# Attention scores computed one head at a time on 64-row, 32-column parts of the TensorE array

## The chip, the core and the metric

The kernel runs on one core of one Trainium2 chip. The metric is device time in microseconds (us) of one execution; lower is better. The engines named below are PE (TensorE, the matrix engine; its weight loads are the separate track PEld), DVE (VectorE), ACT (ScalarE), POOL (GpSimd) and SP (SyncE, which here only issues transfers).

## What is computed

A chunked attention is followed by a gated feed-forward layer. The attention has 4 batches, 8 heads, 768 positions and a head size of 64. Every chunk of 32 queries sees 8 memory keys, 16 keys to the left of the chunk, its own 32 and 8 to the right, 64 keys in all. Everything is float32.

```python
scores = scale * np.matmul(q_c, k_full.transpose(0, 1, 3, 2))   # per chunk: 32 queries x 64 keys
scores = scores - np.max(scores, axis=-1, keepdims=True)
a = np.exp(scores)
a = a / (np.sum(a, axis=-1, keepdims=True) + 1e-09)
out[:, :, c_start:c_end] = np.matmul(a, v_full)
...
xn = x / rms * rms_g                     # x: 3072 tokens x 512
g = xn @ w_gate                          # 512 x 1536
silu = g * (1.0 / (1.0 + np.exp(-g)))
val = xn @ w_val
return (silu * val @ w_out)              # 1536 x 512
```

## The kernel before

Tokens are worked in 8 blocks of 384 (`HT`). The attention of a block is 4 units (`units`, 32 in all); a unit is one batch, one half of the sequence and one pair of heads, so 12 chunks (`NC`) of 32 queries for two heads.

One unit goes through these stages. `stage_ta` and `stage_tb` (L287, L292) transpose queries and keys with DVE into `qb` and `kw` (in the later blocks these are parts of the tiles `qp` and `kv`). `stage_tc` (L300, L301) copies neighbouring keys with ACT. `stage_s` (L309) multiplies queries by keys into the PSUM tile `s`. `stage_ma` and `stage_mb` take the maximum `mx` (L330) and subtract it into `pe` (L336) on DVE, `stage_e` (L341) takes the exponential on ACT, `stage_p` (L348) transposes the result on PE into `pT`, `stage_c` copies that into `pt` (also part of `qp`), and `stage_o` (L368) multiplies by the values into `o`. The two heads of a pair lie on top of each other: head 0 on partitions 0 to 63, head 1 on 64 to 127.

In `qb` the queries of a chunk are 128 partitions by 64 columns: columns 0 to 31 are head 0 and hold numbers on partitions 0 to 63 only, columns 32 to 63 are head 1 and hold numbers on partitions 64 to 127 only. The rest is zero, set once at the start. So one multiplication over 128 partitions gives both heads' scores. `s` has four quarters of 32 partitions: chunks whose `par` is 0 write partitions 0 to 63, those whose `par` is 1 write 64 to 127; `par` changes after every two chunks.

The operands are plain float32, and every multiplication of `stage_s` shows in the trace as two weight loads (LDWEIGHTS) and two MATMULs: 12 chunks give 24 of each for a unit.

The feed-forward part takes its weights and activations as pairs of rounded halves (`xh`, `xl`, `wh_*`, `wl_*`): `moe_in` (L561) makes `pg` and `pv` with 12 MATMULs each, `moe_out` (L599) adds 9 MATMULs into `po` for the step before, and `moe_h` makes `t`, `hh` and `hl` (L568, L572, L575, L584, and the copy in L227) on ACT and DVE.

The first two blocks' attention (8 units) runs in an order that is written out token by token (`ORDER`); its PE also runs multiplications of zeros (`warm`, L307) between the stages. From then on a scheduler orders the work: attention of the next block is put into the feed-forward of the current one in visits (`attn_visits`), and the instructions of PE keep their program order (`on_pe`). A visit runs, on PE, `stage_p` of the unit before, `stage_s` of this unit and `stage_o` of the unit two before, as far as there is one. So of the 4 score stages of a later block two are followed at once by `stage_o`. The scheduler orders DVE and ACT by the dependences that it sees between tiles.

Of the kernel before, what the change touches and what calls it, by code (L numbers as in the profile page):

```python
# [19 lines left out]
CH = 32  # L20
LC, RC = 16, 8
KC = NM + LC + CH + RC
# [45 lines left out]
def tile_kernel(ctx: ExitStack, tc: tile.TileContext, q, k, v, mem_k, mem_v,  # L68
                w_gate, w_val, w_out, rms_g, out):
    nc = tc.nc  # L70
# [35 lines left out]
    def on_pe(ins):  # L106
        if pinned:
            tc.keep_in_program_order(ins)

    def psum_a(name):  # L110
        return psa.tile([P, 512], F32, name=name, tag="at")
# [22 lines left out]
    def which(u):  # L134

        return 1 + u % 2 if u < NE else 0
# [172 lines left out]
    def stage_s(u):  # L309
        d = st[u]  # L310
        qb = qbs[which(u)]
        s = psum_a(f"s{u}")
        hf = units[u][1]
        kw = d["kw"][:, hf:hf + NC]
        for c in range(NC):
            i, par, cp = c // 4, (c // 2) % 2, c % 2
            o = (2 * i + cp) * KC
            on_pe(nc.tensor.matmul(s[64 * par:64 * par + 64, o:o + KC],  # L318
                             lhsT=qb[:, c].rearrange("p s q -> p (s q)"), rhs=kw[:, c], start=True, stop=True))
        d["s"] = s  # L320

    def stage_m(u):
# [357 lines left out]
    for e in range(2):  # L680
        r = slice(64 * e, 64 * e + 64)
# [6 lines left out]
    def attn_visits(blk, x):  # L688


        us = list(range(blk * NG, (blk + 1) * NG))
        for n in range(NG + 2):
            with tc.high_priority():
                if 1 <= n <= NG:
                    stage_p(us[n - 1])
                if n < NG:
                    u = us[n]
                    stage_s(u)
                if n >= 2:
                    stage_o(us[n - 2])  # L700
                    stage_r(us[n - 2], x)
                if n < NG:
                    stage_m(u)
                    stage_e(u)
                if 1 <= n <= NG:
                    stage_c(us[n - 1])
                if n < NG and u + 1 < len(units):
                    stage_t(u + 1)
            if n >= 2 and us[n - 2] + 1 < len(units):
                load_v(us[n - 2] + 1)  # L710
            if n < NG and u + 2 < len(units):
                load_qk(u + 2)
            yield
        with tc.high_priority():
            stage_n(x)
        yield
# [75 lines left out]
    def tok_o(n):  # L792
# [10 lines left out]
        V=lambda n, e=None: stage_v(n, e or ("d" if n < NG else "a")),  # L803

        S=stage_s, M=stage_ma, a=stage_mb, E=stage_e, P=stage_p,
        C=lambda n, e="a": stage_ch(n, 0, e), m=lambda n, e="a": stage_ch(n, 1, e),
        O=stage_o, X=stage_ra, x=stage_rb, u=tok_u,
# [121 lines left out]
```

## Time and profile before

| | us |
|---|---|
| median of 3 runs (732.32 to 733.74) | 733.04 |
| the profiled execution | 731.54 |
| its span, first to last instruction | 729.8 |
| PE busy in the span | 715.1 (98%) |
| DVE busy | 380.0 (52%) |
| ACT busy | 287.8 (39%) |
| POOL busy | 36.4 (5%) |

PE is busy in nearly the whole span, but MATMULs overlap in the records: a record is longer than the distance to the next one's start. What a stage costs is read from where the next stage starts, not from the sum of its records. The 32 score stages have 768 MATMULs, of which the 24 later units have 576.

### The profile page before, as it was taken

What the parts mean: (1) busy time and instruction counts of PE and PEld (TensorE: products, weight loads), DVE (VectorE), ACT (ScalarE), POOL (GpSimd) and SP (SyncE); (2) the same over time, 40 slices, a digit from 0 to 9 for tenths busy, and PEclk for the clock granted to TensorE, in tenths of its full rate; (3) what the DMA queues carried; (4) which work ended last, traced back from release to release, by engine and by line L of the source; (5) the groups of instructions that cost most, each with busy time, mean ns of one, the idle gap of its engine ahead of it and who ended that gap; (6) DMA issues with size and microseconds to landing.
All of it is one profiled execution on the core that took longest, in us unless ns stands there. A gap on an engine that the chain in (4) does not pass through costs nothing.

```text
span 729.8 us, 13052 instructions
## 1 busy us (share of the span) xinstructions
PE 715.1 (98%) x5136; PEld 656.6 (90%) x5136; DVE 380.0 (52%) x725; ACT 287.8 (39%) x600; POOL 36.4 (5%) x143
## 2 busy tenths in 40 slices
PE   8889999999999999999999999999999999999997
PEld 7778999999989999899999999989998999999996
DVE  4888999865645443444535353445434543332222
ACT  4899676643452323422333232432234222341112
POOL 3300000001000000000000000000000000000000
PEclk8999999999999999999999999999999999999999
DMA  8994563414412320122212123021311210010001
GB/s 173 203 259 141 173 202 116 132 37 102 85 37 68 55 50 22 62 46 42 43 38 66 23 45 61 20 66 31 66 29 34 64 32 20 20 44 0 1 1 43
DMA packets 143173, 50.20 MB, mean 69 GB/s; under 512 B 126984, under 2 KB 134536, under 8 KB 143112
## 3 DMA queue, kind: packets, MB, share of 16 engines
q1 hardware_dynamic: 139832, 44.49, 26.6%
q10 hardware_dynamic: 3280, 4.88, 1.8%
q8 instruction: 40, 0.66, 0.4%
q14 instruction: 21, 0.17, 0.1%
HBM read 43.06 MB, written 6.29 MB: 68 GB/s over the span
## 4 chain that ended last, share of the span: by engine, by line
PE 92%; ACT 3%; DMA 3%; DVE 1%; issue 0%; POOL 0%; ACTq 0%; SPq 0%; POOLq 0%
PE pv L561 28%; PE po L599 28%; PE pg L561 27%; PE s L318 3%; PE o L368 3%; PE xT L440 1%; PE pT L348 1%; DMA ws<-in_moe_w_val_dram 1%; DMA memV<-in_mem_v_dram 1%; DMA vw<-in_v_dram 1%; ACT junk L398 0%; ACT ws L508 0%; ACT pt L227 0%; DMA kv<-in_v_dram 0%; ACT qb L227 0%
## 5 line engine op out<-in xcount | busy, mean ns | idle before, releaser
L561 PE MATMUL pv<-xh,wh_v 128*128 128x384 f32 x384 | 132.8, 346 | 0.0
L561 PE MATMUL pg<-xh,wh_g 128*128 128x384 f32 x384 | 129.7, 338 | 0.7 <-DVE t L572 0.7
L561 PE MATMUL pv<-xh,wl_v 128*128 128x384 f32 x384 | 129.5, 337 | 0.6 <-DVE wl_v L532 0.6
L561 PE MATMUL pg<-xh,wl_g 128*128 128x384 f32 x384 | 129.5, 337 | 0.0
L561 PE MATMUL pg<-xl,wh_g 128*128 128x384 f32 x384 | 129.3, 337 | 0.0
L561 PE MATMUL pv<-xl,wh_v 128*128 128x384 f32 x384 | 129.3, 337 | 0.0
L572 DVE SCALAR_TENSOR_TENSOR t<-t,pg 128x384 f32<-128x384 f32 x96 | 53.1, 553 | 138.6 <-ACT t L568 138.5
L227 ACT CAST hh<-t 128x384 fp32r<-128x384 f32 x95 | 48.7, 512 | 174.9 <-PE po L599 165.3
L599 PE MATMUL po<-wh_o,hh 128*128 128x512 f32 x285 | 113.8, 399 | 0.3
L599 PE MATMUL po<-wh_o,hl 128*128 128x512 f32 x285 | 113.1, 397 | 0.0
L599 PE MATMUL po<-wl_o,hh 128*128 128x512 f32 x285 | 112.1, 393 | 0.0
L584 DVE TENSOR_TENSOR hl<-t,hh 128x384 fp32r<-128x384 f32 x95 | 52.9, 557 | 100.7 <-ACT hh L227 95.7
L568 ACT ACTIVATE t<-pg 128x384 f32<-128x384 f32 x96 | 47.2, 492 | 135.9 <-PE pg L561 130.8
L575 DVE TENSOR_TENSOR t<-t,pv 128x384 f32<-128x384 f32 x95 | 52.5, 552 | 64.9 <-PE pv L561 64.4
L561 PEld LDWEIGHTS pg<-xh,wh_g 128*128 128x128 f32 x384 | 72.1, 188 | 4.4 <-DVE t L572 0.9
L561 PEld LDWEIGHTS pg<-xl,wh_g 128*128 128x128 f32 x384 | 72.1, 188 | 3.6
L561 PEld LDWEIGHTS pv<-xh,wh_v 128*128 128x128 f32 x384 | 72.1, 188 | 2.4
L561 PEld LDWEIGHTS pv<-xh,wl_v 128*128 128x128 f32 x384 | 72.2, 188 | 0.9 <-DVE wl_v L532 0.9
L561 PEld LDWEIGHTS pv<-xl,wh_v 128*128 128x128 f32 x384 | 72.2, 188 | 0.3
L561 PEld LDWEIGHTS pg<-xh,wl_g 128*128 128x128 f32 x384 | 72.1, 188 | 0.0
L599 PEld LDWEIGHTS po<-wh_o,hl 128*128 128x128 f32 x285 | 53.5, 188 | 14.1 <-DVE hl L584 1.8
L599 PEld LDWEIGHTS po<-wh_o,hh 128*128 128x128 f32 x285 | 53.5, 188 | 10.0 <-ACT hh L227 1.7
(112 smaller groups left out, 772.9 us busy)
## 6 DMA issues: line engine op xcount, KB each, us to landing
kn<-in_k_dram SPq DMA_DIRECT2D x96, 52.0 KB
qn<-in_q_dram SPq DMA_DIRECT2D x96, 48.0 KB
out_dram<-ob ACTq DMA_DIRECT2D x18, 256.0 KB
ws<-in_moe_w_gate_dram SPq DMA_DIRECT2D x4, 1024.0 KB
ws<-in_moe_w_val_dram SPq DMA_DIRECT2D x4, 1024.0 KB
ws<-in_moe_w_out_dram SPq DMA_DIRECT2D x4, 1024.0 KB
kv<-in_v_dram SPq DMA_DIRECT2D x48, 84.0 KB
kv<-in_v_dram SPq DMA_DIRECT2D x48, 70.0 KB
```

The source lines that it names most:

```text
L227: return nc.scalar.copy(out, in_)
L318: on_pe(nc.tensor.matmul(s[64 * par:64 * par + 64, o:o + KC], lhsT=qb[:, c].rearrange("p s q -> p (s q)"), rhs=kw[:, c], start=True, stop= ...
L348: on_pe(nc.tensor.transpose(out=t[:, i * P:(i + 1) * P], in_=pe[:, i * P:(i + 1) * P], identity=ident))
L368: on_pe(nc.tensor.matmul(o[64 * par:64 * par + 64, c0:c0 + D + 1], lhsT=pt[:, i, 2 * par + hh].rearrange("p c q -> p (c q)"), rhs=d["v"][: ...
L440: on_pe(nc.tensor.transpose(out=t[:, i * P:(i + 1) * P], in_=tiles[i][:, kt * P:(kt + 1) * P], identity=ident))
L561: on_pe(nc.tensor.matmul(ps[:, 0:HT], lhsT=weight(a, n, f, kt), rhs=xs[c][:, kt], start=cnt == 0, stop=cnt == 3 * NKT - 1))
L568: nc.scalar.activation(t, g, AF.Tanh, scale=0.5)
L572: nc.vector.scalar_tensor_tensor(out=t, in0=t, scalar=1.0, in1=g, op0=ALU.add, op1=ALU.mult)
L575: nc.vector.tensor_tensor(out=t, in0=t, in1=vv, op=ALU.mult)
L584: nc.vector.tensor_tensor(out=hl, in0=t, in1=hh.bitcast(F32), op=ALU.subtract)
L599: on_pe(nc.tensor.matmul(po[i], lhsT=h[a][:, i * P:(i + 1) * P], rhs=weight(c, "o", f), start=f == 0 and n == 0, stop=f == NF - 1 and n == 2))
```

## The change

`stage_s` no longer multiplies both heads at once. For each chunk it issues two multiplications, one for each head. Head `hh` reads partitions 64·`hh` to 64·`hh`+63 of keys and of its own 32 query columns, and writes 32 partitions of `s`, the same ones as before. The numbers in `s` are those of before; the zeros in `qb` are no longer read.

```diff
         for c in range(NC):
             i, par, cp = c // 4, (c // 2) % 2, c % 2
             o = (2 * i + cp) * KC
-            on_pe(nc.tensor.matmul(s[64 * par:64 * par + 64, o:o + KC],
-                             lhsT=qb[:, c].rearrange("p s q -> p (s q)"), rhs=kw[:, c], start=True, stop=True))
+            for hh in range(2):
+
+                r, w = slice(64 * hh, 64 * hh + 64), 64 * par + 32 * hh
+                on_pe(nc.tensor.matmul(s[w:w + CH, o:o + KC], lhsT=qb[r, c, hh], rhs=kw[r, c], start=True, stop=True))
         d["s"] = s
```

So the four quarters of `s` now belong to four parts of the array: rows 0 to 63 with columns 0 to 31 (head 0, `par` 0), rows 64 to 127 with columns 32 to 63 (head 1, `par` 0), rows 0 to 63 with columns 64 to 95 (head 0, `par` 1) and rows 64 to 127 with columns 96 to 127 (head 1, `par` 1). Before there were two parts: all rows with columns 0 to 63 and all rows with columns 64 to 127. Lines after L318 move down by two or three.

On PE the stages keep their places. The third visit of the first scheduled block shows it; `pT` is `stage_p`, `s` is `stage_s`, `o` is `stage_o`, and `po` is the feed-forward's output. Before:

```order
L348 MATMUL pT_2178<-ident,pe_2112 128x128 x3
L318 MATMUL s_2182<-kv,qp 64x64 x12
L368 MATMUL o_2195<-kv,qp 64x65 x12
L599 MATMUL po_1031<-wh_o_1310,hh 128x512
L599 MATMUL po_1031<-wl_o_1311,hh 128x512
```

The changed kernel at the same place:

```order
L350 MATMUL pT_2298<-ident,pe_2232 128x128 x3
L321 MATMUL s_2302<-kv,qp 32x64 x24
L370 MATMUL o_2327<-kv,qp 64x65 x12
L601 MATMUL po_1127<-wh_o_1406,hh 128x512
L601 MATMUL po_1127<-wl_o_1407,hh 128x512
```

The row of `s` has 24 multiplications with 32 output partitions instead of 12 with 64; nothing stands in another place.

On DVE the scheduler now sees that each half of `qp` is read by one head's multiplications, and orders differently. The first two visits of that block, before (`mx` and `pe` belong to the unit's scores, the two `qp` transposes and the `kv` transpose to the next unit, `t` and `hl` to the feed-forward):

```order
L330 TENSOR_REDUCE mx_2036<-s_2023 128x6
L287 STREAM_TRANSPOSE qp<-qn_1964 64x12x32 x2
L584 TENSOR_TENSOR hl<-t,hh 128x384
L292 STREAM_TRANSPOSE kv<-kn_1965 128x13x32
L336 TENSOR_TENSOR pe_2038<-s_2023,mx_2036 128x384
L572 SCALAR_TENSOR_TENSOR t<-t,pg 128x384
L575 TENSOR_TENSOR t<-t,pv 128x384
L230 COPY qp<-pT_2093 64x12x32
L330 TENSOR_REDUCE mx_2110<-s_2097 128x6
L287 STREAM_TRANSPOSE qp<-qn_2049 64x12x32 x2
L336 TENSOR_TENSOR pe_2112<-s_2097,mx_2110 128x384
L292 STREAM_TRANSPOSE kv<-kn_2050 128x13x32
```

The changed kernel at the same place:

```order
L287 STREAM_TRANSPOSE qp<-qn_2060 64x12x32
L332 TENSOR_REDUCE mx_2144<-s_2119 128x6
L287 STREAM_TRANSPOSE qp<-qn_2060 64x12x32
L292 STREAM_TRANSPOSE kv<-kn_2061 128x13x32
L586 TENSOR_TENSOR hl<-t,hh 128x384
L338 TENSOR_TENSOR pe_2146<-s_2119,mx_2144 128x384
L574 SCALAR_TENSOR_TENSOR t<-t,pg 128x384
L577 TENSOR_TENSOR t<-t,pv 128x384
L230 COPY qp<-pT_2201 64x12x32
L287 STREAM_TRANSPOSE qp<-qn_2157 64x12x32
L332 TENSOR_REDUCE mx_2230<-s_2205 128x6
L287 STREAM_TRANSPOSE qp<-qn_2157 64x12x32
```

Head 0's half of the next queries is transposed ahead of `mx`, and in these visits `hl` and `pe` stand one or two places later or earlier. On ACT one `t` and one `pe` move by two places in the same two visits.

## Rows read from the trace of the kernel before

**Rows 1.** The page's first part: busy time of each engine over the span.

```profile
span 729.8 us, 13052 instructions
PE 715.1 (98%) x5136; PEld 656.6 (90%) x5136; DVE 380.0 (52%) x725; ACT 287.8 (39%) x600; POOL 36.4 (5%) x143
```

**Rows 2.** The chain that ended last, shares of the span by engine.

```profile
PE 92%; ACT 3%; DMA 3%; DVE 1%; issue 0%; POOL 0%; ACTq 0%; SPq 0%; POOLq 0%
```

**Rows 3.** Busy time by stretch: bounds, length, engines with instruction counts, clock, DMA.

```profile
0.00:57.00 57.00, 48.81 (x684) 43.27 (x684) 40.64 (x86) 42.53 (x93) 12.87 (x52) 0.94 0.95 211
...
212.00:640.00 428.00, 427.79 (x3043) 392.72 (x3042) 192.24 (x390) 137.69 (x315) 16.91 (x68) 1.00 0.20 43
```

**Rows 4.** Groups by line and shape: rows*columns of the array, moved operand, busy, mean ns.

```profile
L318 PE MATMUL s<-kv,qp 128*64 128x64 f32 x576 | 23.2, 228 | 0.0
...
L318 PE MATMUL s<-kw,qb 128*64 128x64 f32 x192 | 8.3, 239 | 3.7 <-POOL kw L221 2.5 <-POOL vw L229 1.0
...
L307 PE MATMUL warm<-zero 128*64 128x64 f32 x64 | 4.7, 224 | 0.0
...
L678 PE MATMUL pm<-ident,mkn 64*128 64x64 f32 x4 | 0.4, 228 | 0.1
```

**Rows 5.** PE in order of time around a later score stage (start, us).

```profile
220.52 0.34 PE L561 MATMUL pg<-xl,wh_g 128*128 128x384 f32 x1
220.70 0.34 PE L561 MATMUL pg<-xh,wl_g 128*128 128x384 f32 x1
220.97 0.97 PE L318 MATMUL s<-kv,qp 128*64 128x64 f32 x24
221.86 0.45 PE L561 MATMUL pv<-xh,wh_v 128*128 128x384 f32 x1
222.14 0.34 PE L561 MATMUL pv<-xl,wh_v 128*128 128x384 f32 x1
222.32 0.34 PE L561 MATMUL pv<-xh,wl_v 128*128 128x384 f32 x1
```

**Rows 6.** PE in order of time in a visit with all three stages.

```profile
179.89 0.49 PE L348 MATMUL pT<-ident,pe 128*128 128x128 f32 x3
180.31 0.97 PE L318 MATMUL s<-kv,qp 128*64 128x64 f32 x24
181.05 0.92 PE L368 MATMUL o<-kv,qp 128*64 128x65 f32 x24
181.90 0.50 PE L599 MATMUL po<-wh_o,hh 128*128 128x512 f32 x1
182.24 0.39 PE L599 MATMUL po<-wl_o,hh 128*128 128x512 f32 x1
182.47 0.40 PE L599 MATMUL po<-wh_o,hl 128*128 128x512 f32 x1
```

**Rows 7.** PE in order of time, early: stages with one part of the array.

```profile
39.34 0.49 PE L240 MATMUL qT<-ident,qf 96*64 96x96 f32 x4
39.67 0.52 PE L237 MATMUL kT<-ident,kf 104*128 104x104 f32 x4
40.03 0.52 PE L240 MATMUL kT<-ident,kf 104*64 104x104 f32 x4
...
46.20 1.21 PE L307 MATMUL warm<-zero 128*64 128x64 f32 x18
```

**Rows 8.** PE in order of time in the first 30 ns of a score stage.

```profile
220.97 0.28 PE L318 MATMUL s<-kv,qp 128*64 128x64 f32 x2
```

**Rows 9.** One line's records: durations in ns, minimum, median, maximum.

```profile
L318 PE MATMUL s<-kv,qp x576: 222/222/271, 166.9 to 607.3; 128*64 128x64 f32 x192
```

**Rows 10.** DVE in order of time in the first scheduled visits.

```profile
173.79 0.56 DVE L330 TENSOR_REDUCE mx<-s 128x6 f32<-128x384 f32 x1
174.27 1.17 DVE L287 STREAM_TRANSPOSE qp<-qn 64x384 f32<-64x384 f32 x2
175.46 0.56 DVE L336 TENSOR_TENSOR pe<-s,mx 128x384 f32<-128x384 f32 x1
176.59 0.61 DVE L292 STREAM_TRANSPOSE kv<-kn 128x416 f32<-128x416 f32 x1 [0.57 <-DMA kn<-in_k_dram]
177.13 0.52 DVE L584 TENSOR_TENSOR hl<-t,hh 128x384 fp32r<-128x384 f32 x1
```

**Rows 11.** ACT in order of time in the same visits.

```profile
176.11 0.53 ACT L341 ACTIVATE pe<-pe 128x384 f32<-128x384 f32 x1
```

## The prediction

> **What bounds the kernel now.** I read the busy shares first: PE is busy in 98% of the span, DVE in 52%, ACT in 39% [rows 1]. The chain that ended last runs over PE for 92% [rows 2]. By stretch this splits in two. From 212 to 640 us PE's records cover 427.79 of 428.00 us, so there every ns that a stage gives or takes on PE goes into the end; in the first 57 us PE is busy for 48.81 only [rows 3]. The score stage is small: 576 MATMULs of the 24 later units and 192 of the 8 early ones [rows 4]. Their busy time, 23.2 and 8.3 us, is not what they cost, because records overlap. The cost is read from starts: a later score stage starts at 220.97, the work behind it at 221.86, so 0.89 us [rows 5]; where stage_o follows, it starts at 181.05 after a score stage that started at 180.31, 0.74 us [rows 6].
>
> **How the 24 MATMULs of a stage run now.** The group of 24 lasts 0.97 us and one record 0.222 us [rows 5, 9], so 24 starts are spread over 0.75 us: 0.75/23 = 33 ns from one to the next. The multiplications of zeros have the same shape, but all write one part of the array: 18 in 1.21 us with records of 224 ns give (1.21 − 0.22)/17 = 58 ns from one to the next [rows 4, 7]. So one part takes a MATMUL every 58 ns, and the score stage keeps two parts going at once: 12 steps of 58 ns are 0.70 us, and the rest of the 0.75 is the start. The first 30 ns of a stage show it too: two MATMULs have started there [rows 8]. In program order the first four belong to the first part, so PE looked past them to fill the second.
>
> **Part 1: twice as many MATMULs, on four parts.** A unit now has 48 MATMULs and 48 weight loads, 12 for each of four parts. If the four run at once as the two do now, the stage is again 12 steps long. The step itself: no row has 32 columns of weights. The transposes are the rows that vary the width. The kT transposes with 128 columns of weights take 0.36 us for four (39.67 to 40.03), those of qT with 64 columns 0.33 us (39.34 to 39.67) [rows 7]; the operand moved through is 104 and 96 columns, so 90/104 = 0.87 and 82/96 = 0.86 ns for a moved column, whatever the weights' width. The scores move 64 columns at 58/64 = 0.91 ns. So the step goes with the moved operand, which stays 64 columns wide. I take 58 ns again, and zero for this part. Its upper bound is that the parts don't all run at once, its lower that the step falls with the columns of weights; both are rivals below. Small ends inside the forecast: two more parts must be started, two take up to 30 ns [rows 8], so at most +0.03 us for a stage; weights half as wide may be in place sooner, at most the 271 − 222 = 49 ns that the first record of a stage is longer than the others [rows 9], of which half is −0.025. These cancel to within ±0.03 us, for 24 stages ±0.7 us. That a MATMUL on 64 rows is not shorter is shown by the transposes on 64 rows: 228 ns against 222 [rows 4, 9].
>
> **Part 2: a new layout next to stage_o.** In 12 places (two visits in each of six blocks) the score stage runs straight into stage_o, and both now use the array as two parts of 64 columns: 0.74 us from start to start, which is the spread of the 24 starts and nothing more [rows 6]. After the change the layouts differ. Upper bound: a score stage that runs into the feed-forward takes 0.89 us, 0.15 more, and the MATMUL behind it then takes 0.28 to the next, where 0.18 is usual, 0.10 more [rows 5]; half of that second loss belongs to the other kind of operand, so 0.20 in all. Lower bound, nothing: kT goes from 128 columns to 64 at 40.03 with no gap, four every 0.36 us on either side [rows 7]. The second row changes the layout but not the kind of work, as here; the first changes both. Neither is nearer in the rows of the array, which only this change touches, so I take the middle, 0.10: 12 × 0.10 = +1.2 us, bounds 0 and +2.4.
>
> The Trainium skill, "TensorEngine Tiling (Array Packing)", section "Tiling Modes", says that changing the tiling mode drains TensorE. The rows of the transposes don't show it, those of the score stage before the feed-forward do; by that rule the 12 places would cost the full upper bound, +2.4 us.
>
> **Part 3: the 8 early units.** PE is idle for 57.00 − 48.81 = 8.2 us of that stretch [rows 3], so a change of a stage there is worth between nothing and its whole. Seven more neighbours differ in layout there (four transposes, two stage_o, one multiplication of zeros): at 0.10 each 0.7 us; I take 0.2.
>
> **Part 4: DVE and ACT in another order.** I cost it at nothing. One 64-partition transpose (1.17/2 = 0.58 us) now stands ahead of mx, but pe stood behind both transposes before as well, so the exponential and the next stage_p hang on the same work: pe ended at 176.0, the exponential at 176.64, and PE transposes it at 179.89, 3.2 us later [rows 6, 10, 11]. hl ended at 177.65, and the po that reads hl starts at 182.47, 4.8 us later [rows 6, 10]. If that cover were gone, a place would cost its 0.6 us, in the two visits where the order changes most 1.2 us.
>
> **Sum.** 0 + 1.2 + 0.2 + 0 = +1.4 us: 731.5 for the profiled execution becomes 732.9. That execution lies 1.5 us below the median of the three runs, so on their scale it is 733.0 + 1.4 = 734.4 us, 732.3 to 736.8 with the bounds above.
>
> **Rivals.**
>
> Rival 1, slower: the two heads take turns. They use different halves of the rows and write one PSUM bank; no row of before has two row halves at work. For it: nothing in the trace shows that row halves overlap. Against it: the two column parts write one bank at once already. If head 0's and head 1's parts alternate, a stage has 24 steps instead of 12: 12 × 58 = 0.70 us more, for 24 stages 16.8, early 8 × 0.70 × one half = 2.8, with the layout's 1.4 together +21: 754 us. It decides soon: one extra step of 58 ns for a stage is 1.4 us in 24. With steps of 45 ns (below) it would be 24 × 45 − 700 = 0.38 us, 9.1 + 1.5 + 1.4 = +12: 745 us.
>
> The Trainium skill, "TensorEngine Tiling (Array Packing)", section "Restrictions and Gotchas", says that different row tiles cannot access the same PSUM bank at the same time. Here they would be in different partitions of it, and no run shows yet whether the rule then holds; by it the result is rival 1's.
>
> Rival 2, slower for another reason: PE doesn't start MATMULs fast enough. Four parts at 58 ns need one every 15 ns; the most that a stage of before sustains is one in 29 (58/2). If that is the limit, the price is rival 1's, 754 us. Against it: two start in less than 30 ns [rows 8].
>
> Rival 3, faster: the step falls with the columns of weights. 58 ns is also (64 + 64) columns at 2.4 GHz plus 5 ns, so half the weights could save 13 ns: 11 steps, −0.145 us for a stage, 24 stages −3.5, early −0.6, layout +1.4: −2.7, 730.3 us. Against it are the transposes [rows 7].
>
> Rival 4: no overlap at all: 48 steps of 58 ns, 2.1 us more for a stage, 24 stages 50, early 8, about 793 us. That it does nothing it says is excluded by the order on PE, which has 24 where 12 stood.
>
> **How the numbers follow.** Forecast 0.55; rival 1 0.18, rival 2 0.06, rival 3 0.16, rival 4 0.05. Faster, same and slower are parted at 0.2% (1.5 us), about what a measurement of this kernel tells from no change. Within the forecast (−0.7 to +3.8, middle +1.4) I give 0.1 faster, 0.5 same, 0.4 slower; rival 3 is faster in 0.85 and the same in 0.15; rivals 1, 2 and 4 are slower. Faster: 0.055 + 0.136 = 0.19. Same: 0.275 + 0.024 = 0.30. Slower: 0.22 + 0.29 = 0.51. The forecast alone holds 732.3 to 736.8. For 8 in 10 the range goes down to 729.5 (most of rival 3) and up to 754 (rivals 1 and 2 up to their middle): 0.55 + 0.13 + 0.14 = 0.82.
>
> **What would show it.** Part 1: the group of 48 at the stage that started at 220.97 lasts 0.9 to 1.0 us, and the pv behind it starts 0.85 to 0.93 us after it; 1.6 us or more is rival 1 or 2 (two records in the first 30 ns and steps of 58 for rival 1, an even 29 for rival 2), 0.74 or less is rival 3. Part 2: stage_o starts 0.8 to 0.95 us after the score stage where it was 0.74. Part 4: no new wait of PE on hl, pe or t. Wrong would be the forecast if the later score stages change by more than 0.1 us each, or if PE waits for DVE in the visits.

## The result and the profile after

The changed kernel took 735.08 us (median; 733.47 to 736.49) against 731.90 us for the kernel before, run beside it on the same chip: a ratio of 1.0037, 95% interval 1.0022 to 1.0052, or +2.7 us (1.6 to 3.8). The time lies in the forecast's range and the sign is as forecast, at about twice the +1.4 us. Most of the loss came from a place to which the prediction gave 0.2 us.

The page of the changed kernel, first part and shares of the chain, against [rows 1, 2]: PE has 768 MATMULs more and the same busy share; the chain has one per cent more each of DVE and "issue" and one less of DMA.

```profile
span 734.4 us, 14609 instructions
...
PE 716.5 (98%) x5904; PEld 656.4 (89%) x5904; DVE 380.6 (52%) x725; ACT 288.2 (39%) x600; POOL 36.4 (5%) x143
...
PE 92%; ACT 3%; DMA 2%; DVE 2%; issue 1%; POOL 0%; ACTq 0%; SPq 0%; POOLq 0%
```

**The score stages.** PE of the changed kernel in order of time, first around a later score stage as in [rows 5], then in a visit with all three stages as in [rows 6] (columns: start, us, engine, line, operation, tiles, rows*columns of the array, moved operand, count):

```profile
225.09 0.34 PE L563 MATMUL pg<-xh,wl_g 128*128 128x384 f32 x1
225.36 0.90 PE L321 MATMUL s<-kv,qp 64*32 64x64 f32 x48
226.19 0.44 PE L563 MATMUL pv<-xh,wh_v 128*128 128x384 f32 x1
226.47 0.34 PE L563 MATMUL pv<-xl,wh_v 128*128 128x384 f32 x1
```

```profile
184.38 0.49 PE L350 MATMUL pT<-ident,pe 128*128 128x128 f32 x3
184.80 0.90 PE L321 MATMUL s<-kv,qp 64*32 64x64 f32 x48
185.63 0.92 PE L370 MATMUL o<-kv,qp 128*64 128x65 f32 x24
186.48 0.50 PE L601 MATMUL po<-wh_o,hh 128*128 128x512 f32 x1
```

Twice the MATMULs take no longer. The group of 48 lasts 0.90 us where the 24 lasted 0.97; ahead of the feed-forward the next stage starts after 0.83 us (226.19 − 225.36) instead of 0.89; ahead of `stage_o` after 0.83 (185.63 − 184.80) instead of 0.74. One line's durations, minimum, median and maximum in ns, beside [rows 9]:

```profile
L321 PEld LDWEIGHTS s<-kv,qp x1152: 102/107/107, 171.6 to 611.7; 64*32 64x32 f32 x192
L321 PE MATMUL s<-kv,qp x1152: 216/216/241, 171.6 to 611.8; 64*32 64x64 f32 x192
```

A record is 216 ns instead of 222, and 0.90 − 0.216 leaves 0.68 us for the 48 starts: one every 14.5 ns, 58 ns for each of four parts, or 56 where the single records of a stage are lined up (they start 30, 7, 12 and 7 ns apart, over and over). In the old stage the second part falls back in the middle, from 13 to 54 ns behind the first; in the new one the last part ends 44 ns behind the first.

Taken over all 24 later units, the stage is 0.068 us shorter in the 12 places ahead of the feed-forward and 0.079 us longer in the 12 ahead of `stage_o` (medians 0.896 to 0.828 and 0.749 to 0.828). Together that is 12 × 0.011 = +0.13 us, which is nothing. And from the first MATMUL of the feed-forward to the end the profiled executions are equal: 729.8 − 51.80 = 678.0 us before, 734.4 − 56.57 = 677.8 after.

**The first 57 us.** So the whole difference of the profiled executions (4.6 us) stands ahead of the first `pg`, which starts at 56.57 instead of 51.80. Busy time by stretch of the changed kernel (columns as in [rows 3]):

```profile
0.00:57.00 57.00, 45.01 (x829) 39.44 (x830) 37.14 (x82) 38.34 (x83) 12.86 (x52) 0.91 0.93 201
212.00:640.00 428.00, 427.79 (x3517) 391.82 (x3517) 192.13 (x386) 138.44 (x311) 16.84 (x68) 1.00 0.20 43
...
45.00:50.00 5.00, 2.41 (x46) 2.10 (x45) 2.14 (x4) 2.29 (x3) 0.00 (x0) 1.00 1.16 261
50.00:57.05 7.05, 5.91 (x68) 5.49 (x69) 5.28 (x14) 4.94 (x8) 0.00 (x0) 0.52 0.91 323
```

The same stretches of the kernel before:

```profile
45.00:50.00 5.00, 3.74 (x65) 3.30 (x64) 4.37 (x9) 4.35 (x7) 0.00 (x0) 1.00 1.10 317
50.00:57.00 7.00, 7.00 (x100) 6.56 (x97) 6.72 (x12) 6.79 (x14) 0.00 (x0) 1.00 0.72 245
```

From 212 to 640 us PE is as full as it was. In the first 57 us PE does 145 more MATMULs in 3.8 us less busy time; from 45 to 50 DVE and ACT do about half of what they did and PE two thirds, and from 50 to 57.05 the granted clock is 0.52, close to the lower of its two levels (1.2 of 2.4 GHz), where it was full. PE's longest wait over the whole run (us in total, times, longest), and PE in that stretch up to the first `pg`:

```profile
PE pT L350 <- DVE r L388: 3.7, 1, 3.7
```

```profile
51.14 0.87 PE L350 MATMUL pT<-ident,pe 128*128 128x128 f32 x3 [3.73 <-DVE r L388]
...
56.57 0.64 PE L563 MATMUL pg<-xh,wh_g 128*128 128x384 f32 x1
```

The same places in the kernel before:

```profile
48.67 0.52 PE L348 MATMUL pT<-ident,pe 128*128 128x128 f32 x3 [1.26 <-DVE r L386]
...
51.80 0.42 PE L561 MATMUL pg<-xh,wh_g 128*128 128x384 f32 x1
```

The multiplications of zeros ahead of this wait begin at 46.20 us, as they did [rows 7]; the wait of `pT` on `r` was 1.3 us before and is 3.7 now. So PE was on time until there, and in this execution the 4.8 us divide in two: `pT` starts 2.5 us later, and from it to the first `pg`, mostly at the lower clock, 5.4 us pass instead of 3.1. DVE of the changed kernel shows what `r` stood behind:

```profile
48.84 1.23 DVE L520 SCALAR_TENSOR_TENSOR ws<-ws 128x1024 uint32<-128x1024 uint32 x1 [2.86 <-ACT ws L510]
...
50.91 0.18 DVE L388 RECIPROCAL r<-r 128x6 f32<-128x6 f32 x1
```

DVE idled 2.86 us for ACT's work on `ws`, here the second part of the gate weights (the fourth transfer of weights), and `r` comes after that in its queue. ACT in turn waits for the transfer of `ws`, here in the changed kernel:

```profile
47.71 1.10 ACT L510 ACTIVATE ws<-ws 128x1024 int32<-128x1024 uint32 x1 [2.96 <-DMA ws<-in_moe_w_gate_dram]
```

and here in the kernel before:

```profile
45.17 1.19 ACT L508 ACTIVATE ws<-ws 128x1024 int32<-128x1024 uint32 x1 [0.39 <-DMA ws<-in_moe_w_gate_dram]
```

That step starts 2.54 us later because SP issued the transfer 2.31 us later. SP's queue in the changed kernel (start, time that the issues took, count):

```profile
34.65 1.71 SPq L211 DMA_DIRECT2D vw<-in_v_dram  x2
36.40 1.06 SPq L205 DMA_DIRECT2D vw<-in_v_dram  x1
37.51 2.90 SPq L211 DMA_DIRECT2D vw<-in_v_dram  x4
40.45 0.42 SPq L205 DMA_DIRECT2D vw<-in_v_dram  x1
40.92 0.88 SPq L211 DMA_DIRECT2D vw<-in_v_dram  x2
41.90 0.39 SPq L498 DMA_DIRECT2D ws<-in_moe_w_gate_dram  x1
```

and in the kernel before:

```profile
34.12 0.81 SPq L211 DMA_DIRECT2D vw<-in_v_dram  x2
34.97 0.42 SPq L205 DMA_DIRECT2D vw<-in_v_dram  x1
35.44 2.65 SPq L211 DMA_DIRECT2D vw<-in_v_dram  x4
38.13 0.42 SPq L205 DMA_DIRECT2D vw<-in_v_dram  x1
38.59 0.89 SPq L211 DMA_DIRECT2D vw<-in_v_dram  x2
39.59 0.39 SPq L496 DMA_DIRECT2D ws<-in_moe_w_gate_dram  x1
```

The lists are the same. An issue mostly takes 0.42 us; the kernel before has one of 1.03 (in the third row), the changed kernel one of 1.35 (first row), one of 1.06 (second row) and one of 1.50 us (third row), and its list begins 0.53 us later. What else was going on then shows in the DMA queues from 33.5 to 43.5 us (packets, MB, share of 16 engines), changed kernel:

```profile
q1 hardware_dynamic: 3513, 1.18, 61.8%
q8 instruction: 2, 0.03, 1.4%
q14 instruction: 2, 0.02, 0.9%
```

The kernel before has no row of q8 there. Queue 8 seems to bring PE's instructions: the pages count 40 such packets before and 46 after, each of 16 KB, and PE has 2 × 5136 instructions before and 2 × 5904 after, which is 257 to a packet in both. The early score stages hold 192 MATMULs and 192 weight loads more, so the fetches fall at other places. The two in this stretch begin at 34.8 and 38.9 us, and the two longest issues at 35.0 and 38.9.

### The profile page after: what moved, and what is told of

Its sections match the earlier page's. It is cut to its first block, busy times and chain, and to the rows that moved or that the text cites. A ratio compares the mean times of both kernels' runs of the same rounds, so it can differ in the third digit from the quotient of the medians.

```text
span 734.4 us, 14609 instructions
## 1 busy us (share of the span) xinstructions
PE 716.5 (98%) x5904; PEld 656.4 (89%) x5904; DVE 380.6 (52%) x725; ACT 288.2 (39%) x600; POOL 36.4 (5%) x143
## 4 chain that ended last, share of the span: by engine, by line
PE 92%; ACT 3%; DMA 2%; DVE 2%; issue 1%; POOL 0%; ACTq 0%; SPq 0%; POOLq 0%
PE pv L563 28%; PE po L601 27%; PE pg L563 27%; PE o L370 3%; PE s L321 3%; PE pT L350 1%; PE xT L442 1%; DMA ws<-in_moe_w_gate_dram 1%; DMA memV<-in_mem_v_dram 1%; ACT junk L400 0%; ACT qb L227 0%; ACT wy L511 0%; DVE kw L230 0%; DMA kv<-in_v_dram 0%; PE po L629 0%
```

## The experiments

Of the lines of `ORDER`, and of diffs with many lines, only the part that changes is shown. The theory after this reading, A: the later units cost nothing, and the loss is early, where more instructions on PE delay the start of the feed-forward. Its rival, B: the later score stages cost the 1 to 3 us by their layout, and the start differs from run to run. "First pg" below is the start of the feed-forward in the profiled execution (51.80 before, 56.57 after); "the later part" is the time from there to the end (678.0 and 677.8).

**The change in the 24 later units alone**, and **in the 8 early units alone**. `NE` is 8; the second has `u < NE` in place of `u >= NE`.

```diff
+            if u >= NE:
+                for hh in range(2):
+                    r, w = slice(64 * hh, 64 * hh + 64), 64 * par + 32 * hh
+                    on_pe(nc.tensor.matmul(s[w:w + CH, o:o + KC], lhsT=qb[r, c, hh], rhs=kw[r, c], start=True, stop=True))
+            else:
+                on_pe(nc.tensor.matmul(s[64 * par:64 * par + 64, o:o + KC],
+                                 lhsT=qb[:, c].rearrange("p s q -> p (s q)"), rhs=kw[:, c], start=True, stop=True))
```

> The change in the 24 later score stages alone; the 8 early ones as before. Theory A (from the trace after: 12 later stages that run into the feed-forward are 0.07 us shorter each, 12 that run into stage_o cost 0.08 us more each, so the later part is worth 12 x (0.08 - 0.07) = +0.1 us, and the rest of the loss arises in the first 57 us): ratio 0.999 to 1.001 to the kernel before. Rival (the later stages carry the loss, 2.7 us / 24 = 0.11 us each): ratio 1.003 to 1.004.

> The change in the 8 early score stages alone. Theory A: the whole loss is here, ratio 1.002 to 1.005, and feed-forward starts 2 to 5 us later than the 51.8 us of before. Rival (later stages): 0.999 to 1.001.

Measured: later units alone 1.0001 (0.9991 to 1.0012); early units alone 1.0026 (1.0014 to 1.0037), +1.9 us. First pg at 52.51 and 55.76, later parts 678.1 and 678.2. B falls: the later units' 576 MATMULs became 1152 at +0.1 us (−0.7 to +0.9), and the 8 early stages hold the loss.

**The changed kernel again**, to see whether the late start belongs to it.

> The changed kernel once more, on the same chip as the three others, for the start of the kernel. Theory A1 (the early loss is a steady effect of the change): feed-forward starts at 56 to 57 us again, ratio 1.003 to 1.005. Rival A2 (the start varies from run to run, whatever the kernel): another start time, 52 to 57 us, and a ratio that may be 1.000 to 1.005.

Measured: 1.0027 (1.0012 to 1.0042), first pg 55.04, the weights issued at 41.69. The late start is steady, its size is not: single runs lie between 731.4 and 737.0 us. With the same order of tokens, the profiled executions of the three kernels whose early score stages have two parts (before, later units alone, and the next one) reach the first pg at 51.80 to 53.24, those of the six with four parts (the changed kernel twice, early units alone, and three below) at 53.90 to 58.70. Over the twelve runs the mean span was 732.96 us at a mean granted clock of 0.9942, that of the kernel before 731.09 us at 0.9965.

**`stage_o` split in the same way**, in the later units: 64 of its 128 rows and 32 columns, so that it has the layout of the new score stage.

```diff
+                    if u >= NE:
+                        for cp in range(2):
+                            r, w = slice(64 * cp, 64 * cp + 64), 64 * par + 32 * cp
+                            on_pe(nc.tensor.matmul(o[w:w + CH, c0:c0 + D + 1], lhsT=pt[r, i, 2 * par + hh, cp],
+                                                   rhs=d["v"][r, 2 * i + par, hh, :], start=True, stop=True))
```

> In the 24 later units both the scores and stage_o work on 64 rows and 32 columns at a time, so there is no change of layout between them; early units as before. Theory (the boundary's 0.14 us is the change of layout, the step falls from 58 to 56 ns): the score stage ahead of stage_o is 0.69 us from start to start instead of 0.83 in the kernel after; 24 x 0.07 = 1.7 us and stage_o about 24 x 0.02 = 0.5 us saved: ratio 0.997, 729.5 to 730.5 us where the kernel before has 732. Rival (the boundary is not the layout but the half rows): still 0.8 us from start to start, ratio 1.000 to 1.003.

Measured: 0.9971 (0.9961 to 0.9981), −2.1 us: faster than both kernels. PE in a visit with all three stages:

```profile
181.93 0.49 PE L353 MATMUL pT<-ident,pe 128*128 128x128 f32 x3
182.35 0.90 PE L321 MATMUL s<-kv,qp 64*32 64x64 f32 x48
183.04 0.89 PE L376 MATMUL o<-kv,qp 64*32 64x65 f32 x48
183.86 0.50 PE L610 MATMUL po<-wh_o,hh 128*128 128x512 f32 x1
```

The score stage ahead of `stage_o` now costs 0.69 us (183.04 − 182.35) instead of 0.83 in the changed kernel: with the same layout on both sides the new neighbour costs nothing. The gain adds up from medians: 12 × 0.055 ahead of `stage_o`, 12 × 0.068 ahead of the feed-forward, and 24 × 0.030 in `stage_o` itself (0.849 to 0.819), together 2.2 us. The profiled execution, the slowest of the eleven, does not show all of it: its first pg is at 53.24 and its later part 677.2 us, 0.8 less than before, since one `stage_o` at 193 us, which waits for values, took 2.30 us where it was 1.19.

**32 columns, all 128 rows**: each head on its own columns, the zeros of the other still multiplied (a single run).

```diff
+            for hh in range(2):
+                w = 64 * par + 32 * hh
+                on_pe(nc.tensor.matmul(s[w:w + CH, o:o + KC], lhsT=qb[:, c, hh], rhs=kw[:, c], start=True, stop=True))
```

> Each head on all 128 rows (zeros included) and 32 columns: four parts of the array that lie side by side, as many MATMULs as after. Theory (the step of a part follows the 64 moved columns, and four parts run at once whether rows are halved or not): a later score stage is as long as after, 0.83 us to the feed-forward, 0.90 us as a group; the boundary to stage_o stays at about 0.83. Rival (half the rows are what makes the step 56 instead of 58 ns): 0.87 us or more.

PE in a visit, one group of scores ahead of `stage_o`:

```profile
182.58 0.90 PE L320 MATMUL s<-kv,qp 128*32 128x64 f32 x48
183.41 0.92 PE L369 MATMUL o<-kv,qp 128*64 128x65 f32 x24
```

The same 0.90 and 0.83 us, a total of 734.01 us and a first pg at 54.55. The stage behaves as it does because of the four column parts; that a head uses half of the rows changes nothing here. The change of columns costs the same with and without a change of rows; a change of rows alone was not run.

**Head by head in order**: the 12 chunks of head 0, then the 12 of head 1 (a single run). It asks what lets four parts run at once.

```diff
-        for c in range(NC):
-            ...
-            for hh in range(2):
+        for hh in range(2):
+            for c in range(NC):
```

> The multiplications of the changed kernel in another order: all 12 chunks of head 0, then all of head 1, so that in program order only two parts of the array have work near each other. Theory (PE looks ahead only some MATMULs past those that wait, about four for a part): the stage takes nearly twice the 0.83 us, 1.3 to 1.5 us from start to start, some 15 us in all, 747 to 753 us. Rival (PE looks ahead over the whole stage, or the two row halves would have overlapped anyway): 0.8 to 0.9 us, no change in time.

```profile
225.01 1.39 PE L320 MATMUL s<-kv,qp 64*32 64x64 f32 x48
226.33 0.44 PE L562 MATMUL pv<-xh,wh_v 128*128 128x384 f32 x1
```

The stage costs 1.32 us instead of 0.83, the later part 690.1 us instead of 678: 12.1/24 = 0.50 us for a stage. The total, 745.67 us, is a little short of what was expected; the length of the stage is as expected. Now only two parts at a time have MATMULs close together in program order, and about two run at once (48 starts over 1.18 us, 25 ns apart, where one part needs 56). The four parts run at once because the code alternates between the heads.

**What makes the start late.** The next kernels vary one link each. In the early order's tokens `W18` is 18 multiplications of zeros, `S0` the first unit's score stage, and `Z` the issue of the next weight transfer. The first kernel moves the fetches of the kernel before: 26 multiplications of zeros, 104 instructions, at two places where PE is idle.

```diff
-K0a Q1a S0 p2
+K0a Q1a W18 S0 p2
-X3 S4
+X3 W8 S4
```

> The score stages as before; 26 more multiplications of zeros (104 PE instructions) in two places of the first 31 us where PE was idle (18 ahead of the first score stage, 8 ahead of the fifth). Theory F (a 16 KB fetch of PE instructions makes a transfer that SP issues at that moment take 1.3 to 1.9 us instead of 0.42, and the twice as long score stages move two more such fetches into the 34 to 42 us in which SP issues without a pause): the fetch that fell at 44.4 us in the kernel before comes at 37 to 40 us, one of SP's issues beside it takes over 1.2 us, the gate weights are issued 0.8 to 1.5 us later than 39.6 us, ratio 1.0005 to 1.002, with no change in the score stage. Rival G (the new layout itself slows the start): no issue of SP over 1.1 us between 34 and 42 us, ratio 0.999 to 1.0005.

Measured: 1.0008 (0.9998 to 1.0019). The fetch moved from 44.4 to 36.9 us, into SP's issues; the issue beside it took 1.07 us, and the weights were issued at 38.75, no later than before. This speaks neither for the fetches nor clearly against them; the profiled execution was the fastest of its eleven.

**More instructions alone**: the kernel before with 84 tiny multiplications of zeros (4 columns each), 336 instructions, in two idle places, nothing else changed (`G60` is 60 of them).

```diff
+    def pad(n):
+        w = pmw[0]
+        for i in range(n):
+            j = 32 * (i % 4)
+            nc.tensor.matmul(w[j:j + 32, 0:4], lhsT=zero[:, 0:32], rhs=zero[:, 0:4], start=True, stop=True)
-K0a Q1a S0
+K0a Q1a G60 S0
-K6d t6
+K6d G24 t6
```

> The score stages as before, all with 64 columns. Added are 84 small multiplications of zeros (336 PE instructions, as many as the change adds by 39 us) in two places where PE sat idle: 60 ahead of the first score stage (idle 2.45 us), 24 ahead of the queries' transpose at 34.9 us (idle 0.8 us). Theory F (it is the fetches of PE's instructions among SP's issues): two fetches fall between 33 and 43 us as in the kernel after, one or two of SP's issues beside them take over 1.2 us, the gate weights are issued at 41 to 42.5 us where it was 39.6, feed-forward starts at 54 to 56.5 us, ratio 1.002 to 1.004. Rival G (the new layout slows the start by itself): gate weights issued by 40.9 us, feed-forward by 53.3, ratio 0.999 to 1.001.

Measured: 1.0015 (1.0004 to 1.0027), +1.1 us, with score stages that are those of before; this lies between the two ranges that were expected. The added MATMULs fit into the idle time: the first score stage starts at 11.46, where it was 11.31. Two fetches stand among SP's issues, at 36.7 and 40.9, beside issues of 1.42 and 1.27 us; the weights are issued at 42.56 and first pg is at 55.08. But the start was late already. PE, early, in this kernel (in brackets the idle time ahead of the group and what ended it):

```profile
15.51 0.73 PE L240 MATMUL kT<-ident,kf 104*64 104x104 f32 x3 [2.51 <-issue]
```

PE had stood for 2.51 us in "issue", waiting for nothing that the profile shows, with a fetch that began at 12.8. So instructions cost time here beyond their MATMULs, and the profile shows two places where they may: SP's issues and PE's own "issue".

**The early weight transfer moved ahead**: the token that issues it stands before `w4` instead of after `K5d`, in the changed kernel and in the kernel before.

```diff
-X3 S4 x3 w4 u3 t5
+X3 S4 x3 Z w4 u3 t5
-Y0 K5d Z K6d
+Y0 K5d K6d
```

> The changed kernel, with the fourth transfer of weights (the gate weights that ACT waits for at 45 us) issued ahead of five transfers of values instead of behind them. Theory F: the fetches still lengthen SP's issues, but the gate weights are no longer behind both; they are issued by 38 us, ACT takes them by 45 us, feed-forward starts at 52 to 54 us, and the ratio to the kernel before falls to 0.998 to 1.001. Rival G (PE's own work at the start is slower): feed-forward still starts at 55 us or later, ratio 1.002 or more.

> The kernel before with the same transfer moved. It measures what that move is worth where no fetch falls among SP's issues: theory F: the gate weights land 1 to 2 us sooner, of which the start gives back 0 to 1 us (another wait is next): ratio 0.9985 to 1.000. If it gains as much as the changed kernel gains (2 us or more), the move and not the fetch is what the kernel after_z shows.

Measured: the changed kernel with the move 1.0018 (1.0004 to 1.0032), the kernel before with it 0.9998 (0.9989 to 1.0008). The profiled execution of the first did as expected (weights issued at 37.75, first pg at 51.58), but its later part is 679.7 us, since the next weights came later in turn (ACT waits 1.64 us for them), and most of its runs are slower than that one. The kernel before loses what the move gains in the same way (51.09 and 679.3). Against 1.0027 and 1.0037 without the move the interval decides nothing.

**The clock**: the changed kernel with 26 instead of 9 multiplications of zeros in the idle stretch, to hold the clock up.

```diff
-L O4 B2a f W9 X4
+L O4 B2a f W26 X4
```

> The changed kernel with 17 more multiplications of zeros (2.0 us) at 46 us, where PE then sat idle for 3.7 us and the granted clock was 0.5 from 50.2 us on. Theory H (half of the loss is the half clock that follows that idle time): no stretch at 0.5 between 45 and 60 us, feed-forward starts 1 to 2 us sooner than in the kernel after (54 to 55.5 us), ratio to the kernel before 1.0005 to 1.0025. Rival (the transfer is what all waits for, the clock costs nothing): feed-forward at 55 to 56.6 us as after, ratio 1.0025 to 1.004.

Measured: 1.0021 (1.0009 to 1.0033). In the profile the granted clock stays full there and first pg is at 53.28; but in that execution the weights had been issued at 39.12. Over the twelve runs the mean granted clock was 0.9969, as in the kernel before (0.9966 beside it), and the mean span 732.60 us against 731.28. With the clock of before the loss is still 1.3 us of about 1.9, unless the added multiplications cost something themselves. That points to the clock as the smaller part; the intervals overlap too far to call it shown, and in the profile of the changed kernel the stretch at the lower clock held 2.3 of the 4.8 us.

**Both stages split in all 32 units**, which doubles `stage_o`'s early instructions as well.

> Scores and stage_o on 64 rows and 32 columns in all 32 units, the early ones too. The later part gains what the kernel with both in the later units alone gained (0.29%, 2.1 us). Theory F: the early stage_o add 384 PE instructions to the 384 of the scores, SP's issues are lengthened again, the start is 2 to 5 us later: ratio 0.999 to 1.004. Rival G (only the layout's change between stages costs, and there is less of that here): ratio 0.997 to 0.9985.

Measured: 1.0053 (1.0038 to 1.0068), +3.9 us, above what was expected. The later part is the shortest of all, 675.7 us, and first pg the latest, 58.70. PE of this kernel ahead of the feed-forward:

```profile
47.40 0.66 PE L371 MATMUL o<-vw,pt 64*32 64x65 f32 x31
51.38 0.70 PE L371 MATMUL o<-vw,pt 64*32 64x65 f32 x17 [3.33 <-issue]
52.01 2.18 PE L307 MATMUL warm<-zero 128*64 128x64 f32 x18
```

and its waits for instructions alone, out of those of the whole run:

```profile
PE o L371 <- issue: 3.3, 1, 3.3
...
PE kT L237 <- issue: 2.1, 1, 2.1
PE pT L349 <- issue: 1.3, 1, 1.3
...
PE warm L307 <- issue: 1.0, 1, 1.0
```

PE stops for 3.33 us in the middle of a stage, with a fetch (48.9 us) and the weight transfers running; the kernel before has no such wait. Against the 2.1 us that the later units gained by the split, the early ones lose some 6 (3.9 + 2.1), 4.1 more than with the scores alone split there. PE's waits on "issue" are the sign that the instructions are the cause; the split of the early `stage_o` alone was not run.

## Why the prediction came out as it did

**Part 1 held**, and a little more than that. Four parts run at once, each with a step of 56 ns (taken: 58), so twice the MATMULs are free. I had set the start of two more parts against the weights' earlier arrival and put ±0.03 us as bounds; the stage gained 0.068, beyond them. From the starts in the traces, 27 ns of it are the first step of a part (80 instead of 107 ns; taken for the weights' earlier arrival: 25), 25 are the ten steps after it (55.8 instead of 58.3 ns; taken: nothing), 10 are the last part's lag behind the first (44 instead of 54 ns; taken: 30 more), and 6 the gap to the next stage (146 instead of 152).

**Rivals 1, 2 and 4 fall.** Heads that take turns would have made a group of 1.6 us; it lasted 0.90. A limit of one start in 29 ns fails at one in 14.5. Rival 3 falls too: the step is 56 ns with 32 columns of weights, not 45, as the transposes had said [rows 7].

The Trainium skill, "TensorEngine Tiling (Array Packing)", section "Restrictions and Gotchas", says that different row tiles cannot access the same PSUM bank at the same time. The trace does not agree for different partitions of a bank: the 48 MATMULs, half of them on either half of the rows and all writing one bank, keep a step of 56 ns on all four parts, as do those that use all rows.

**Part 2's price was about right, but it has a counterpart that the sum lacked.** The row of `stage_o` starts 0.079 us later in each of 12 places, taken was 0.10. Taken apart, the gap between the last start of the scores and the first of `stage_o` grew from 4 to 146 ns, toward the upper bound of 0.20 us, and the shorter spread of the starts gave nearly half of it back. So +0.95 us here stand against −0.82 ahead of the feed-forward, which Part 1 had at zero: the two together make +0.13 us where the sum had +1.2.

The Trainium skill, same page, section "Tiling Modes", says that changing the tiling mode drains TensorE. The runs agree: the gap of 146 ns stands where the columns of a part change from 32 to 64, and with equal layouts it is gone (0.69 us from stage to stage instead of 0.83). The early transposes, which go from 128 to 64 columns with one part at work, show no such gap in either kernel: 89 ns from start to start across the change as within a stage.

**Part 3 is the step that was mis-sized.** I took 0.2 us, from a bound that held only PE's own stages: their whole length at most, since PE idles for 8.2 us there. The early units measured +1.9 us (1.0 to 2.7) alone. What the step left out is that a stage's cost can lie in its instructions and not in its MATMULs. 384 instructions more move and add fetches; PE waits for "issue" by itself (0.4 us in the changed kernel, 2.5 with the padding, 7.7 in the four waits shown with both stages split), and SP's issues ahead of the gate weights took longer. These weights come 2.5 us later, ACT waits in front of them, PE stands idle, and the granted clock then falls to 0.52: the profile's 4.8 us at the first pg. The idle 8.2 us, by which I bounded what a stage there can cost, were no such bound, since some of them end on a chain that starts at SP.

**Shown and not shown.** Shown: the loss lies in the early stages; the later part is equal; more instructions, with the same score stages, cost 1.1 us (0.3 to 2.0); more still cost more. Only seen together: SP's long issues and the fetches. Over the 14 traces, from 5 to 50 us, 28 of the 107 issues that overlap a fetch of queue 8 took over 1.2 us, and 7 of the 691 others, six of them issues of the `w_out` weights. In the changed kernel's second profile (26.4 us, 1.44 us; 38.3 us, 1.88 us) and in the one with early units alone (26.6, 35.3 and 39.8 us, 1.47 to 1.90 us) each begins within 0.5 us of a fetch. Against it stand an issue of 2.0 us with no fetch near it, while a weight transfer ran (at 40.3 us in the kernel before with the token moved), and the moved fetch that cost SP only 1.07 us. Open: how the 1.9 us divide between SP's delay, PE's own wait for instructions and the clock.

**Part 4 held**: in the visits PE has no new wait on `hl`, `pe` or `t`, and from 212 to 640 us it idles for 0.21 us as before.

So that the measured +2.7 us lies inside the forecast's bounds around +1.4 is partly luck: +1.2 expected in the later units where +0.1 was found, 0.2 in the early ones where 1.9 to 2.6 was.

## What to carry to other kernels

In this kernel a block diagonal with zeros cost no more than its split into parts of the array, since the step of a part followed the moved columns; a split pays where the stages around it share its layout, and where the code alternates between the parts. Where PE already runs without a gap, count a change in MATMULs by starts; where it waits for transfers, count its instructions too, and keep the change out of that stretch: the split of both stages in the later units alone was the only version that was faster, by 0.29%.

## What the runs showed of the hardware that was not expected

Four parts of the array, 64 rows by 32 columns each, run float32 MATMULs at the same time and write one PSUM bank: a start every 14.5 ns. PE takes MATMULs out of program order for this: in order, two neighbouring MATMULs of one part would hold up the rest for a step, and 24 such steps of 56 ns are 1.3 us. It did not reach as far as the other head's 24 MATMULs: with 12 chunks of one head in a row, which leaves two parts, the 48 starts spread over 1.18 us instead of 0.68.

PE's instructions are a resource. With 336 and 768 more of them in the first 57 us (the padding, both stages split), PE stood for up to 2.51 and 3.33 us at a time for "issue", in the middle of a stage, and the second of these while weight transfers ran. The kernel before shows no such wait, the kernel with the later units alone, whose early stages are the same, one of 1.0 us, and the changed kernel none over 0.2.
